# Reordering the routing and the first items of a linear-attention and expert kernel

## The chip, the cores and the metric

The kernel runs on one core of one Trainium2 chip. A core has five engines [...]: TensorE (PE, matmuls; the loading of its stationary operand is listed as PEld), VectorE (DVE), ScalarE (ACT), GpSimd (POOL) and SyncE (SP, which here only issues DMAs). The metric is the device time of one execution in microseconds (us). Three runs of the kernel before took 386.9, 387.04 and 388.13 us; their median is 387.04.

## The reference

Two blocks follow one another, all in float32. The first is a linear attention with a decayed state (4 batches, 8 heads, 768 tokens, head size 48):

```
for t in range(S):
    cur = einsum('bhd,bhe->bhde', u * k[t], v[t])
    y[t] = einsum('bhd,bhde->bhe', r[t], state + cur)
    state = w * state + einsum('bhd,bhe->bhde', k[t], v[t])
```

Its output, put together over the heads, is `x` (4 x 768 tokens of 384 numbers). The second is a mixture of 8 experts of hidden size 1024. Each token takes its own best expert, or, where a local gate says so, the expert of the token before it:

```
for s in range(S):
    fresh_e = argmax(logits[b, s])
    e = fresh_e if s == 0 or local_gate[b, s] < 0.5 else prev_e
    prev_e = e
    out[b, s] = softmax(logits[b, s])[e] * (relu(x[b, s] @ w1[e]) @ w2[e])
```

## The kernel before

**The attention** works through 16 items, numbered n; an item is one batch and a pair of heads. Its 768 tokens are six chunks of 128. For each item the kernel makes, by name:

- `scale` (POOL): `ke` (keys with their decay to the chunk's end, L217), `pd` (r times k, L221) and from item 3 on `rw` (r with its decay, L234), each as two instructions.
- `keys` (DVE): `kw`, keys over the decay (L241).
- `scores` (PE, L288, and DVE, L290): products of `rw` and `kw`, in two groups g of three chunks; DVE masks them into `am`. The second group's mask is handed back as a function, which `run` calls as `keep()`.
- `own` (PE, L269, and DVE, L273): each token's own term, written to the PSUM tile `y`, then multiplied by v.
- `added` (PE, L253): the sum of k times v of each chunk, into a part of the PSUM tile `mp`; `states` (DVE, L259): a scan over the chunks, which reads these sums and gives the states `S`.
- `inside` (PE, L297): `am` times v, added to `y`; `before` (PE, L310): `rw` times `S`, added to `y`; then ACT copies `y` to `xT` (L314).
- `turn` (PE, L323, and ACT, L325): `xT` transposed back to tokens; after each fourth item ACT sends `x` to memory.
- `logits` and `token_logits` (L336, L342): after each fourth item, the router's logits.

PSUM is tight: there is one `y` tile, so an item's `own` follows the copy of the last item's `y`; and two `pair` tiles, taken in turn by scores, turns and logits, each of which waits for the reader of the one before the last. `ke`, `pd`, `kw`, `am` and `S` have two buffers each. The loads rk (r and k), kv and vT are issued by SP three items ahead.

**The order** is written out by hand in `Attention.run`. [...] From item 5 on the scores are made one item ahead.

**The routing** is woven into the same loop. The tokens are routed in two groups of two batches. The first group's routing (`router...(0)`) runs from item 9 to item 15: `experts_of` finds each token's best expert; `keys` transposes (L690) and `runs` scans (L695) to carry an expert along to later tokens; `turn_runs` (L700, with ACT's copy L701) transposes back; `last` (L707) spreads the last token's result; `one_hot` (L713 to L720), `counts` (L727, L728), `ranks` (L734 to L746), `slots` (L775 to L778), `columns` (L783), `numbers` (L788) and `places` (L794) give each token its place in its expert's list; `summed` (L801), `copied` (L807) and `head` (L811 to L832) make the list of the tokens to gather, and `heads()` starts the gather on POOL (L1048). In `ranks` the places at which the second group's tokens go on are written too (L744, L745). The second group's routing runs in `Experts.routing`, beside the first expert's matmuls.

**The experts** follow: ten units of gathered tokens, each with two matmul stages, the larger ones with fewer products and more sums on DVE. The weights come by DMA two units ahead.

Of the kernel before, what the change touches and what calls it, by code (L numbers as in the profile page):

```python
# [14 lines left out]
Alu = mybir.AluOpType  # L15
# [5 lines left out]
P = 128  # L21
# [5 lines left out]
E, F = 8, 1024  # L27
DK, FK = D // P, F // P
NCH = S // P
NC = B * NCH  # L30
# [7 lines left out]
EARLY = 2  # L38
HEAD = 192
TAIL = 256  # L40
# [10 lines left out]
C2 = NCH // 2  # L51
# [4 lines left out]
def spread(ap, axis, n):  # L56

    a = ap.unsqueeze(axis)
    return a.to_broadcast([n if i == axis else s for i, s in enumerate(a.shape)])


class Attention:
# [145 lines left out]
    def scale(self, n):  # L208

        nc, t = self.nc, self.items[n]  # L210
        t["ke"] = self.two.tile([P, NCH, 2 * DH], F32, name="ke")
        t["pd"] = self.two.tile([P, NCH, P], F32, name="pd")
        t["rw"] = self.four.tile([P, NCH, P], F32, name="rw")
        hp = t["hp"]

        def ke(p):
            nc.gpsimd.tensor_mul(t["ke"][:, p::2], t["k"][:, p::2], spread(self.endT[:, p, hp], 1, C2))  # L217

        def pd(i):
            z = slice(i * C2, (i + 1) * C2)  # L220
            nc.gpsimd.tensor_mul(t["pd"][:, z], t["rT"][:, z], t["kT"][:, z])  # L221

        def rw(i):
            self.decayed(nc.gpsimd, n, slice(i * C2, (i + 1) * C2))


        for what in (pd, ke) if n < 3 else (ke, rw, pd) if n < 5 else (rw, ke, pd):
            for i in range(2):
                what(i)

# [60 lines left out]

    def inside(self, n):
        nc, t = self.nc, self.items[n]
        for c in range(NCH):
            p, c2 = c % 2, c // 2
            for h in range(2):
                nc.tensor.matmul(t["y"][p * DP:(p + 1) * DP, h, c2 * P:(c2 + 1) * P],  # L297
                                 lhsT=t["v"][:, (2 * c + h) * DH:(2 * c + h) * DH + DP],
                                 rhs=t["am"][:, c // 3, h, c % 3], start=False, stop=False, skip_group_check=True)
# [45 lines left out]
    def run(self, router, fetch, heads):  # L345


        def pair(name):
            t = self.banks(name)
            return [t[:, 0], t[:, 1]]  # L350

        M = B * HP

        mp, mp_end = router.mp, 2 * P + 2 + (NCH - 1) * DH

        g = GROUPS[0][1] * HP
        for n in range(M + 1):
            if n + AHEAD - 1 < M:
                self.load(n + AHEAD - 1)
            elif n + 2 == M:  # L360
                fetch()
            if n == 0:
                self.scale(0)
                self.keys(0)
                self.tables()
                self.scores(0, 0)()
                self.scores(0, 1)()
                self.own(0)
                self.nc.scalar.copy(self.first, self.tab[:, 1, 0])
                self.turn_ends(slice(1, HP))  # L370
                self.warm(3)
                self.added(0)
                self.reciprocals(1)
                self.states(0)
                self.scale(1)
                continue
            if n < 3:

                self.keys(n)
                self.inside(n - 1)  # L380
                self.before(n - 1)
                if n == 2:
                    self.turn(0, pair("tp"))
                self.nc.scalar.copy(self.first, self.tab[:, n + 1, 0])
                self.scores(n, 0)()
                keep = self.scores(n, 1)
                self.own(n)
                if n == 1:
                    keep()
                self.added(n)  # L390
                self.states(n)
                if n == 2:
                    keep()
                else:
                    self.reciprocals(2)
                self.scale(n + 1)
                continue
            if n < M:
                self.turn(n - 2, pair("tp"))
                if n == g + 3:  # L400
                    router.turn_runs(0, mp[:, mp_end:])
                if n == g + 4:
                    router.counts(0, [mp, mp[:, E * NC // 2:]])
                if n == 3:
                    self.added(3)
                    self.reciprocals(3)
                if n < 5:
                    self.keys(n)
                if n > 3:
                    self.added(n)  # L410
            if n == g + 3:
                router.last(0, mp[:, mp_end:])
            if n < M:
                self.states(n)
            if n > HP and n % HP == 1:
                self.token_logits(n // HP - 1, pair("lq")[0])
            if n == 3:
                self.chooser()
            if n == g + 1:
                router.experts_of(0, (0,))  # L420
            if n == g + 3:
                router.one_hot(0)
            if n == g + 4:
                router.ranks(0, (0,))
            if n == g + 5:
                router.slots(0)
                router.columns(0)
            if n == g + 6:
                router.numbers(0)
            if n == M:  # L430
                router.shares(0)
            if n + 1 < M:
                self.scale(n + 1)
            if 3 <= n < 6:
                router.constants(n - 3)
            if n == M:
                self.turn(M - 2, pair("tp"))
            self.inside(n - 1)
            self.before(n - 1)
            if n == 6:  # L440
                router.cast()
            if n == M:
                break
            if n == g + 7:

                router.summed(0, 0)
                router.copied(0)

            ahead = n if n < 5 else n + 1
            if ahead < M:  # L450
                self.scores(ahead, 0)()
                keep = self.scores(ahead, 1)
            if n % HP == 0:

                keep()
                self.own(n)
                self.logits(n // HP - 1, pair("lp")[0])
                if n == 4:
                    self.keys(5)
                    self.scores(5, 0)()  # L460
                    self.scores(5, 1)()
                    self.keys(6)
                else:
                    self.keys(n + 2)
                if n == g + 4:
                    router.ranks(0, (1,))
            else:
                self.own(n)
                if 4 < n < M - 2:
                    self.keys(n + 2)  # L470
                if ahead < M:
                    keep()
            if n == g + 1:
                router.experts_of(0, (1,))
            if n == g + 2:
                router.keys(0, mp)
                router.runs(0)
            if n == g + 5:
                router.places(0, 0)
            if n == g + 6:  # L480
                router.places(0, 1)
            if n == g + 7:
                router.head(pair("tb")[0])
                heads()
        self.inner.close()


# [79 lines left out]
class Router:  # L567
# [162 lines left out]
    def ranks(self, i, parts=(0, 1)):  # L730

        nc, g, n = self.nc, self.g[i], self.g[i]["nc"]
# [5 lines left out]
        if 1 in parts:  # L738
            if i == 0:

                nc.vector.tensor_scalar(g["far"], g["pos"][:, :EARLY], float(HEAD), float(TAIL - HEAD), Alu.is_ge, Alu.mult)
                nc.vector.tensor_tensor(g["pos"][:, :EARLY], g["pos"][:, :EARLY], g["far"], op=Alu.add)
                base, end = self.g[1]["ext"][:, :, 0:1], g["exc"][:, :, n:]
                nc.vector.tensor_copy(base, end)  # L744
                nc.vector.tensor_scalar(base[:, :EARLY], end[:, :EARLY], float(TAIL - HEAD), float(TAIL), Alu.add, Alu.max)  # L745
            nc.vector.tensor_tensor(g["pos"], g["pos"], g["oh"], op=Alu.mult)  # L746

    def blocks(self):

# [52 lines left out]
                                  rhs=g["ohq"][:, c], start=(i == 0 and what == 0 and c < 4), stop=True,  # L802
                                  skip_group_check=True)

    def copied(self, what):
        self.rows = self.tl(f"rows{what}", [P, P]) if not hasattr(self, "rows") else self.rows
        self.nc.scalar.copy(self.rows, self.mp[:, what * P:(what + 1) * P])  # L807

    def turned(self, bank):

# [3 lines left out]
    def heads(self, table, out):  # L814
        self.nc.vector.tensor_reduce(out, table[:, :EARLY, :2], axis=AX.X, op=Alu.add)
# [160 lines left out]
class Experts:  # L976
# [345 lines left out]
    def routing(self, s):  # L1322

        r, bank = self.router, self.bank
        if s == 0:
            r.experts_of(1)
            r.shares(1)
            r.gates(0)
        if s == 1:
# [386 lines left out]
```

## Time and profile before

| | |
|---|---|
| median of three runs | 387.04 us |
| profiled execution | 387.78 us |
| its span, first to last instruction | 386.1 us |
| PE busy | 368.5 us, 95% |
| DVE busy | 250.4 us, 65% |
| POOL busy | 150.6 us, 39% |
| attention | about 0 to 118 us |
| experts | about 118 to 380 us |
| HBM traffic | 193 GB/s over the span, 410 GB/s and more in the first 45 us |

A line of the timeline reads: start in us, length in us, engine, line of the kernel, operation, what it writes and reads, shape, count; in brackets the idle time of the engine before it, and who ended that. Lines of one engine that follow one another and are alike are merged. The page's clock row is the share of full clock, in tenths, that TensorE was granted in each of 40 equal slices (9.65 us each).

### The profile page before, as it was taken

What the parts mean: (1) busy time and instruction counts of PE and PEld (TensorE: products, weight loads), DVE (VectorE), ACT (ScalarE), POOL (GpSimd) and SP (SyncE); (2) the same over time, 40 slices, a digit from 0 to 9 for tenths busy, and PEclk for the clock granted to TensorE, in tenths of its full rate; (3) what the DMA queues carried; (4) which work ended last, traced back from release to release, by engine and by line L of the source; (5) the groups of instructions that cost most, each with busy time, mean ns of one, the idle gap of its engine ahead of it and who ended that gap; (6) DMA issues with size and microseconds to landing.
All of it is one profiled execution on the core that took longest, in us unless ns stands there. A gap on an engine that the chain in (4) does not pass through costs nothing. (4 is left out here: it accounts for less than half of the span.)

```text
span 386.1 us, 9699 instructions
## 1 busy us (share of the span) xinstructions
PE 368.5 (95%) x3858; PEld 326.4 (85%) x3858; DVE 250.4 (65%) x718; ACT 107.4 (28%) x293; POOL 150.6 (39%) x212
## 2 busy tenths in 40 slices
PE   7998999989999999999999999999999999999992
PEld 6775777667768998998999999999999999999971
DVE  6887678959944654587557757758757758556400
ACT  4132232313232111322322233234224234222220
POOL 8769999849222031511333212212413213012022
PEclk9999999989999999999999999999999999999998
DMA  7999999969404891740552146145146146064011
GB/s 253 412 411 410 406 371 322 373 233 342 153 22 144 345 361 39 252 185 23 185 184 103 42 170 220 60 171 205 60 180 225 38 166 230 17 208 174 2 37 37
DMA packets 17478, 74.97 MB, mean 194 GB/s; under 512 B 2730, under 2 KB 6587, under 8 KB 14865
## 3 DMA queue, kind: packets, MB, share of 16 engines
q1 hardware_dynamic: 10048, 56.89, 39.6%
q0 software_dynamic: 3424, 9.52, 7.6%
q10 hardware_dynamic: 3952, 7.87, 5.5%
q8 instruction: 32, 0.52, 0.6%
q14 instruction: 22, 0.17, 0.2%
HBM read 64.83 MB, written 9.51 MB: 193 GB/s over the span
## 5 line engine op out<-in xcount | busy, mean ns | idle before, releaser
L1274 POOL DMA_INDIRECT out_dram<-yo,sid x27 | 26.6, 987 | 102.4 <-ACT yo L1269 79.0
L1125 PE MATMUL h<-exT,w1t 128*128 128x168 f32 (+4 forms) x240 | 54.9, 327 | 0.0
L1129 DVE TENSOR_TENSOR hT<-h,hs 128x168 f32<-128x168 f32 (+3 forms) x60 | 21.0, 351 | 46.6 <-PE h L1125 30.5
L1048 POOL DMA_INDIRECT xg<-x_d,gid x29 | 31.1, 1074 | 39.1 <-DVE sm L883 17.4
L1125 PEld LDWEIGHTS h<-exT,w1t 128*128 128x128 f32 x240 | 41.7, 190 | 0.3 <-issue 0.3
L1075 PE MATMUL h<-exT,w1t 128*128 128x192 f32 (+1 forms) x192 | 38.2, 337 | 0.0
L1194 PE MATMUL y<-factors,sums 128*128 128x192 f32 x168 | 36.8, 326 | 0.0
L290 DVE TENSOR_TENSOR am<-pair,kept 128x768 f32<-128x768 f32 x32 | 30.0, 950 | 9.6 <-PE pair L288 9.2
L221 POOL TENSOR_TENSOR pd<-rk 128x384 f32<-128x384 f32 x32 | 31.4, 1000 | 10.8 <-PE y L269 9.6
L1125 PE MATMUL h<-xs,ws 128*128 128x168 f32 (+4 forms) x144 | 35.2, 326 | 0.0
L1075 PEld LDWEIGHTS h<-exT,w1t 128*128 128x128 f32 x192 | 32.3, 190 | 1.4 <-issue 0.2
L1125 PEld LDWEIGHTS h<-xs,ws 128*128 128x128 f32 x144 | 25.5, 190 | 4.3 <-ACT hs L1132 1.2
L1194 PEld LDWEIGHTS y<-factors,sums 128*128 128x128 f32 x168 | 28.9, 190 | 0.0
L297 PE MATMUL y<-am,kv 128*64 128x128 f32 x384 | 26.7, 284 | 0.8 <-DVE y L273 0.8
L217 POOL TENSOR_TENSOR ke<-kv,endT 128x288 f32<-128x288 f32 x32 | 24.9, 798 | 4.4 <-DMA kv<-in_kv_dram 3.2
L288 PE MATMUL pair<-rw,kw 48*64 48x128 f32 (+1 forms) x768 | 22.9, 249 | 2.4 <-DVE kw L241 1.1
L297 PEld LDWEIGHTS y<-am,kv 128*64 128x64 f32 x384 | 23.1, 141 | 1.3 <-DVE y L273 1.2
L314 ACT COPY xT<-y 128x768 f32<-128x768 f32 (+1 forms) x16 | 12.5, 780 | 39.7 <-PE y L310 39.7
L234 POOL TENSOR_TENSOR rw<-rk,tab 128x384 f32<-128x384 f32 x26 | 23.5, 924 | 0.0
L288 PEld LDWEIGHTS pair<-rw,kw 48*64 48x64 f32 x768 | 19.7, 133 | 4.4 <-issue 2.7
L1194 PE MATMUL y<-w2t,hT 128*128 128x192 f32 x96 | 23.0, 328 | 0.0
L1062 DVE COPY exT<-tp 128x384 f32<-128x384 f32 (+6 forms) x29 | 14.0, 488 | 13.6 <-PE tp L1061 13.4
(279 smaller groups left out, 736.3 us busy)
## 6 DMA issues: line engine op xcount, KB each, us to landing
w1t<-in_w_dram SPq DMA_DIRECT2D x9, 1536.0 KB, 6.7
w2t<-in_w_dram SPq DMA_DIRECT2D x9, 1536.0 KB, 7.7
rk<-in_rk_dram SPq DMA_DIRECT2D x15, 768.0 KB, 8.5
kv<-in_kv_dram SPq DMA_DIRECT2D x16, 584.0 KB, 8.1
vT<-in_vT_dram SPq DMA_DIRECT2D x16, 384.0 KB, 8.0
x_d<-x ACTq DMA_DIRECT2D x4, 1152.0 KB, 8.7
w1t<-in_w_dram ACTq DMA_DIRECT2D x1, 1536.0 KB, 11.1
w2t<-in_w_dram ACTq DMA_DIRECT2D x1, 1536.0 KB
```

Of the source, the lines that this page charges most:

```text
L217: nc.gpsimd.tensor_mul(t["ke"][:, p::2], t["k"][:, p::2], spread(self.endT[:, p, hp], 1, C2))
L221: nc.gpsimd.tensor_mul(t["pd"][:, z], t["rT"][:, z], t["kT"][:, z])
L234: engine.tensor_mul(t["rw"][:, z], t["rT"][:, z], spread(pw, 1, z.stop - z.start))
L288: nc.tensor.matmul(sc[f * DP:(f + 1) * DP, h, i, x:], lhsT=t["kw"][q, c, o * DP:(o + 1) * DP], rhs=t["rw"][q, c, x:], start=True, stop=True)
L290: return lambda: nc.vector.tensor_mul(t["am"][:, g], sc, spread(self.kept[:, g:g + 3], 1, 2))
L297: nc.tensor.matmul(t["y"][p * DP:(p + 1) * DP, h, c2 * P:(c2 + 1) * P], lhsT=t["v"][:, (2 * c + h) * DH:(2 * c + h) * DH + DP], rhs=t["am" ...
L1048: self.nc.gpsimd.indirect_dma_start(out=xg[:n], out_offset=None, in_=self.x_d[:rows], in_offset=bass.IndirectOffsetOnAxis(ap=u["gid"][:n, ...
L1075: nc.tensor.matmul(h[:, :n], lhsT=u["w1"][:, m, kk, :], rhs=u["xT"][:, kk, :], start=(kk == 0), stop=(kk == DK - 1))
L1125: nc.tensor.matmul(out, lhsT=a, rhs=b, start=start and k == 0, stop=stop and k == len(terms) - 1, skip_group_check=True)
L1129: nc.vector.tensor_tensor(out, a, b, op=Alu.add)
L1194: return lambda: nc.tensor.matmul(bank[:, x * half:(x + 1) * half], lhsT=a, rhs=b, start=(j == 0 and x == 0), stop=(j == FK // 2 - 1), ski ...
L1274: self.nc.gpsimd.indirect_dma_start(out=out.rearrange("n (h d) -> (n h) d", h=2) if half else out, out_offset=bass.IndirectOffsetOnAxis(ap ...
```

## The change

Five things are reordered in `Attention.run`, and small functions adapted to it.

1. The routing's `keys` and `runs` move up in item 10, right behind own (L269, L273) and ahead of the product `kw` and the second `am`. `turn_runs` moves down, between `inside` and `before`; `last` and the first part of `one_hot` move behind `before`. `states` of item 11 no longer stands behind `last`. The second part of `one_hot` goes to the end of the item, `counts` and the first part of `ranks` move to item 12's end, behind the logits.
2. `kw` of item 5 is made in item 4's step ahead of `inside`, right behind item 4's `kw` and `S`. In item 3, `added` and `states` move behind `own` and `keep()`; in item 2, `keep()` stands ahead of `states`.
3. The start of the second token group's slots (L744, L745) leaves `ranks` and becomes `carried`, called in the experts.
4. In item 3 POOL makes `rw` ahead of `ke`.
5. `inside` goes through the same twelve matmuls, with the two column halves p of the array in turn.

Besides, in item 15 the list's copy (`copied`) is made by DVE instead of ACT, and the list's transpose and the gather are emitted ahead of `own`.

```
-        for what in (pd, ke) if n < 3 else (ke, rw, pd) if n < 5 else (rw, ke, pd):
+        for what in (pd, ke) if n < 3 else (ke, rw, pd) if n == 4 else (rw, ke, pd):
...
-        for c in range(NCH):
-            p, c2 = c % 2, c // 2
-            for h in range(2):
+        for c2, h in [(c2, h) for c2 in range(C2) for h in range(2)]:
+            for p in range(2):
+                c = 2 * c2 + p
                 nc.tensor.matmul(t["y"][p * DP:(p + 1) * DP, h, c2 * P:(c2 + 1) * P],
...
                 self.own(n)
-                if n == 1:
-                    keep()
+                keep()
                 self.added(n)
                 self.states(n)
-                if n == 2:
-                    keep()
-                else:
+                if n == 1:
                     self.reciprocals(2)
...
             if n < M:
                 self.turn(n - 2, pair("tp"))
-                if n == g + 3:
-                    router.turn_runs(0, mp[:, mp_end:])
-                if n == g + 4:
-                    router.counts(0, [mp, mp[:, E * NC // 2:]])
                 if n == 3:
-                    self.added(3)
                     self.reciprocals(3)
                 if n < 5:
                     self.keys(n)
                 if n > 3:
                     self.added(n)
-            if n == g + 3:
-                router.last(0, mp[:, mp_end:])
-            if n < M:
-                self.states(n)
+                    self.states(n)
+            if n == 4:
+                self.keys(5)
...
-            if n == g + 3:
-                router.one_hot(0)
-            if n == g + 4:
-                router.ranks(0, (0,))
...
             self.inside(n - 1)
+            if n == g + 3:
+                router.turn_runs(0, mp[:, mp_end:])
             self.before(n - 1)
...
+            if n == g + 3:
+                router.last(0, mp[:, mp_end:])
+                router.one_hot(0, (0,))
             if n == g + 7:
                 router.summed(0, 0)
-                router.copied(0)
+                router.copied(0, self.nc.vector.tensor_copy)
+                router.head(pair("tb")[0])
+                heads()
...
                 if n == 4:
-                    self.keys(5)
                     self.scores(5, 0)()
                     self.scores(5, 1)()
                     self.keys(6)
-                else:
+                if n == g + 4:
+                    router.counts(0, [mp, mp[:, E * NC // 2:]])
+                    router.ranks(0, (0,))
+                if n > 4:
                     self.keys(n + 2)
                 if n == g + 4:
                     router.ranks(0, (1,))
             else:
                 self.own(n)
+                if n == g + 2:
+                    router.keys(0, mp)
+                    router.runs(0)
+                if n == 3:
+                    self.added(3)
                 if 4 < n < M - 2:
                     self.keys(n + 2)
                 if ahead < M:
                     keep()
+                if n == 3:
+                    self.states(3)
             if n == g + 1:
                 router.experts_of(0, (1,))
-            if n == g + 2:
-                router.keys(0, mp)
-                router.runs(0)
+            if n == g + 3:
+                router.one_hot(0, (1,))
...
-            if n == g + 7:
-                router.head(pair("tb")[0])
-                heads()
...
-                base, end = self.g[1]["ext"][:, :, 0:1], g["exc"][:, :, n:]
-                nc.vector.tensor_copy(base, end)
-                nc.vector.tensor_scalar(base[:, :EARLY], end[:, :EARLY], float(TAIL - HEAD), float(TAIL), Alu.add, Alu.max)
             nc.vector.tensor_tensor(g["pos"], g["pos"], g["oh"], op=Alu.mult)
+
+    def carried(self):
+        nc, n = self.nc, self.g[0]["nc"]
+        base, end = self.g[1]["ext"][:, :, 0:1], self.g[0]["exc"][:, :, n:]
+        nc.vector.tensor_copy(base, end)
+        nc.vector.tensor_scalar(base[:, :EARLY], end[:, :EARLY], float(TAIL - HEAD), float(TAIL), Alu.add, Alu.max)
...
-    def copied(self, what):
+    def copied(self, what, copy=None):
...
-        self.nc.scalar.copy(self.rows, self.mp[:, what * P:(what + 1) * P])
+        (copy or self.nc.scalar.copy)(self.rows, self.mp[:, what * P:(what + 1) * P])
...
         if s == 0:
             r.experts_of(1)
+            r.carried()
             r.shares(1)
             r.gates(0)
```

Here `g` is 8, so that `g + 2` is item 10 and `g + 4` item 12.

## The prediction

> **What bounds the kernel now.** I read the page first: its engine totals, then its clock row.
>
> ```profile
> span 386.1 us, 9699 instructions
> PE 368.5 (95%) x3858; PEld 326.4 (85%) x3858; DVE 250.4 (65%) x718; ACT 107.4 (28%) x293; POOL 150.6 (39%) x212
> ...
> PEclk9999999989999999999999999999999999999998
> ```
>
> TensorE (PE) is the bound from end to end. It is idle for some 8.7 us between its first and last matmul, and the clock drops in one slice in the middle, 77 to 87 us. The chain of waits is no help: it stops at the last scatter. So I went by the timeline of PE, where each idle time stands beside its releaser. The stage view puts 7.47 busy us into the stretch from 76 to 86 us, at a mean clock of 0.83, and 260.2 of 262 us into the experts' stretch from 118 to 380 us. The experts don't change and have nothing to give; the change lives in the attention part, the first 118 us. There the timeline of PE has three places that the diff touches. The first and largest:
>
> ```profile
> 75.52 0.28 PE L690 MATMUL mp<-ident,key 128*12 128x128 f32 x1
> 75.75 0.79 PE L323 MATMUL pair<-ident,xT 112*128 112x112 f32 x6
> 78.78 0.23 PE L700 MATMUL mp<-ident,run 12*128 12x12 f32 x1 [2.23 <-DVE run L695]
> 79.31 1.04 PE L253 MATMUL mp<-kv,ke 128*48 128x48 f32 x20 [0.30 <-issue]
> 80.28 0.60 PE L707 MATMUL mp<-rn,ident 128*128 128x12 f32 x2
> 80.81 2.48 PE L297 MATMUL y<-am,kv 128*64 128x128 f32 x24
> ```
>
> PE's queue is served in order, so the small transpose L700 of the routing's runs holds everything behind it for 2.23 us. After it L253 takes 1.04 and L297 2.48 us, against 0.65 and 1.58 in every other item. DVE shows why `run` is late:
>
> ```profile
> 75.72 0.97 DVE L273 TENSOR_TENSOR y<-y,vT 128x768 f32<-128x768 f32 x1
> 76.59 0.94 DVE L241 TENSOR_TENSOR kw<-rk,inv 128x768 f32<-128x768 f32 x1
> 77.45 0.95 DVE L290 TENSOR_TENSOR am<-pair,kept 128x768 f32<-128x768 f32 x1
> 78.32 0.40 DVE L695 TENSOR_TENSOR_SCAN run<-mp,seg 12x128 f32<-12x128 f32 x1
> ```
>
> The 0.40 us scan stands behind three large products. The second and third place, items 5 and 13, are PE waiting for DVE again:
>
> ```profile
> 34.05 1.11 PE L288 MATMUL pair<-rw,kw 48*64 48x64 f32 x42 [0.52 <-issue]
> ...
> 38.44 1.24 PE L288 MATMUL pair<-rw,kw 48*64 48x128 f32 x48 [1.10 <-DVE kw L241]
> 40.30 0.41 PE L323 MATMUL pair<-ident,xT 112*128 112x112 f32 x2 [0.62 <-DVE am L290]
> ```
>
> ```profile
> 93.87 0.77 DVE L741 TENSOR_SCALAR far<-pos 128x24 f32<-128x24 f32 x1
> 94.67 0.79 DVE L742 TENSOR_TENSOR pos<-pos,far 128x24 f32<-128x24 f32 x1
> 95.39 0.82 DVE L744 COPY ext<-exc 128x8 f32<-128x8 f32 x1
> 96.24 0.72 DVE L745 TENSOR_SCALAR ext<-exc 128x2 f32<-128x2 f32 x1
> ```
>
> The last four delay item 14's `am`, for which PE waits 0.71 us at 99.25.
>
> [...] its clock record has 3.41 us at 0.5 from 79.34 us, after a window of that length in which PE was idle for 2.5 us; idle times of 1.1 us did not do it. [...] L741, L742, L744 and L745 write 128x24 and less and take 0.72 to 0.82 us, each until one of POOL's instructions ends; L746, 128x96, takes 0.24 with POOL idle. [...] four records of L801 start within 20 ns.
>
> **Routing's wait, item 11.** From one item's L323 to the next takes 5.33 us where nothing waits (46.49 to 51.83); here 10.09 (75.75 to 85.84). L700 and L707 must still be issued: about 0.45 us, since L690 holds 0.23 [...]. So up to 10.09 - 5.33 - 0.45 = 4.3 us can go. In the new order the scan is right behind `y` (76.6 to 77.0 us), and L700 behind L253 and L297, thus at about 75.75 + 0.74 + 0.6 + 1.4 = 78.5. Slack 1.5 us: the wait is gone, and the half clock with it. L707 needs ACT's copy of `rn`, 0.17 us, which has before()'s 0.7 us as cover. Next late: the one-hot operations L714 to L716. They now stand ahead of item 12's first `am`, wanted at 80.5; [...] L323 of item 12 would then wait up to 0.6 us. I take 0.3: **-4.0** (-4.3 to -3.6).
>
> **Array halves in turn.** The 24 records of L297 of one item start in pairs 109 ns apart for five pairs, and then singly 57 and 52 ns apart: both halves already work at once, and the new order can't double anything. First to last start is 1.31 us; L801 and L253, whose halves already alternate, stay paired to their end. Kept paired, L297 would need 1.26: -0.05 x 12 items on PE's path = **-0.6** (-0.8 to 0).
>
> **Items 2 to 5.** These steps nearly cancel. Gains: L253 of item 3 no longer waits for `ke` (0.41 us at 24.46); with `rw` first POOL needs only rk, and has `pd` of item 3 at about 26.6 instead of 28.1; kw of item 5 is made before item 4's `am`, so the 1.10 us go. Followed in order: item 3's scores can't start before its `kw` at 27.2 (before: 27.33), so the 0.41 buys 0.1. Own at 28.5, `y` 29.5 to 30.45, second `am` to 31.3, and only then `S` of item 3, now last, to 31.9. But added(4) overwrites the sums that `S` reads, and stands on PE right behind turn(2), ready at 30.7: **a new wait of 1.25 us**, the queue behind it being all of item 4. Then L253 31.95, L297 32.4, L310 33.9, scores 34.5, own 35.8 (behind ACT's xT), logits 36.6, scores of item 5 at 38.0 (before 38.44, kw long ready), first `am` done at 39.9, L323 39.95 against 40.30: -0.35. That has no room for the 0.52 us at 33.5, for which the profile names no releaser; if it comes again, +0.2. I take **-0.1** (-0.5 to +0.5). The swapped `am` and `S` of item 2 cost DVE the same sum.
>
> **Counts and ranks, items 12 and 13.** L744 and L745 leave (1.54 us on DVE); in the experts, with POOL's products over, they take about 0.06 to 0.17 each beside PE's matmuls: nothing. But L735 and L737 (0.63 + 0.26) come behind own(12), and must wait for L727 and L728, now behind the logits: with own(12) starting at T, ACT has copied the counts at T+3.1, L737 ends T+4.0, kw T+5.0, L741 to L746 T+6.4, `S` T+7.05, slots (1.4) T+8.45, `am` T+9.4. Before, L323 came at T+9.21 with the counts' 0.42 us spent ahead of T: a gain of 0.2. Against it L718 and L720 now stand ahead of item 13's `am` while POOL makes `rw`: 0 to 0.6 us, on the logits. Sum **+0.1** (-0.3 to +0.7).
>
> **Item 15.** The rows' copy moves from ACT to DVE (about 0.3 us, as L807's 0.27) and L811 ahead of own(15): own starts at about 110.3 instead of 109.88, and `y` at 111.3 instead of 110.87, behind L815 to L832: +0.4 on the wait at 111.59. The gather starts 1.3 us earlier; the expert's transposes at 116.65 take 0.91 us, which I read as 0.3 of waiting for its second tile: -0.3. Sum **+0.1** (-0.3 to +0.5). SP's loads keep their order; those that wait for buffers are issued earlier with PE's steps, and land 4 us and more before use.
>
> **Sum.** -4.0 - 0.6 - 0.1 + 0.1 + 0.1 = -4.5. The profiled execution took 387.78 us (span 386.1 and 1.7 around it): 383.3. It lies 0.74 above the median of 387.04. If the lower runs escaped the half clock [...], 383.3 stands; if the 0.74 is noise, 382.5. I say **383.1 us**, a ratio of 0.990.
>
> **Rivals.**
> - *Half is given back* (chance 0.2): the wait goes, but the top ends hold: +0.5, +0.7, +0.5 and no gain of the array's halves, with a wait of 0.6 at item 12: -3.6 + 1.7 = -1.9, some 385.5. For it: DVE has 5.8 us of work in items of 5.3 there.
> - [...] (slower, 0.07): the routing's small operations, moved to where POOL always works, each wait for one of its 0.98 us instructions, as L741 to L745 did. Eight of them (L715, L716, L718, L720, L735, L741, L742, L776) at 0.75 us more is 6 us of DVE time ahead of `am` of items 12 to 14; with about 1 us hidden, 5 us on PE, and 0.5 slower: about 388. It decides once more than six are held so. Against: L681, L682 and L746 were not held.
> - *Nothing measurable* (0.08): the median runs had no half clock [...]: near 386.5.
> - *The wait stays*, because `run` is still late: under 0.02, with 1.5 us of slack.
>
> **How the numbers follow.** The main case has 0.65 and 381.5 to 384.8; with half given back, the range is 381.2 to 386.4. A difference within 0.3% (1.2 us) is about what a measurement of this kernel can't tell from none: faster 0.84, same 0.09, slower 0.07.
>
> **What would show it.** Right: no L700 row with idle time, no slice of lower PEclk in the middle, L253 and L297 of item 11 at 0.65 and 1.5 us; an idle time of about 1.2 us before item 4's L253, released by S L259; none before item 5's scores; 0.3 to 0.5 more before inside(15). Wrong: idle times over 1 us before L323 or L336 of items 12 to 14 released by `am`, with small DVE rows of 0.7 to 1 us ahead; L297 unchanged at 1.58; or a second drop of the clock.

## The result and the profile after

Over 22 runs of each the changed kernel takes 385.39 us and the kernel before 387.48 us: a ratio of 0.9941, with a 95% interval of 0.9918 to 0.9964. The ratios here and below leave out a run that met a slower state of the chip, and are not the quotients of two medians. The kernel is faster, by 2.1 us where 4 were forecast. The profiled execution of the changed kernel took 384.17 us against 387.78, and is the fastest of its 22 runs, so the two profiles differ by 3.6 us, more than the medians do. Both gaps, 3.6 against 4.5 and 2.1 against 3.6, have to be explained.

The page of the kernel after, engine totals and clock row:

```profile
span 382.4 us, 9699 instructions
PE 366.8 (96%) x3858; PEld 324.6 (85%) x3858; DVE 249.3 (65%) x719; ACT 107.2 (28%) x292; POOL 150.5 (39%) x212
...
PEclk9999999999999999999999999999999999999998
```

The slice of lower clock in the middle is gone. PE is idle for 6.6 us between its first and last matmul, against 8.7. The timeline of PE around the routing's wait:

```profile
75.46 0.79 PE L323 MATMUL pair<-ident,xT 112*128 112x112 f32 x6
76.69 0.66 PE L253 MATMUL mp<-kv,ke 128*48 128x48 f32 x20 [0.44 <-issue]
77.15 1.53 PE L297 MATMUL y<-am,kv 128*64 128x128 f32 x24
78.92 0.23 PE L700 MATMUL mp<-ident,run 12*128 12x12 f32 x1 [0.25 <-DVE inc L713]
...
82.10 0.79 PE L323 MATMUL pair<-ident,xT 112*128 112x112 f32 x6
```

The wait of 2.23 us before L700 is gone, and L253 and L297 take 0.66 and 1.53 us instead of 1.04 and 2.48. But two short idle times are new: 0.44 us before L253 and 0.25 before L700. DVE shows what ends them:

```profile
76.19 0.40 DVE L695 TENSOR_TENSOR_SCAN run<-mp,seg 12x128 f32<-12x128 f32 x1
76.52 0.92 DVE L241 TENSOR_TENSOR kw<-rk,inv 128x768 f32<-128x768 f32 x1
...
78.23 0.63 DVE L259 TENSOR_TENSOR_SCAN S<-step,mp 128x240 f32<-128x240 f32 x1
```

L695 ends at 76.59, and L253 starts at 76.69. L259 ends at 78.86, and L700 starts at 78.92. Both DVE operations read `mp`, and both matmuls write `mp`, in other columns. The releasers that the profile prints ("issue", `inc`) are not the cause: in all seven profiles with this order L253 starts 0.10 us after L695's end and L700 0.06 us after L259's, while the idle time before L253 varies from 0.44 to 0.72 us.

Items 2 to 5, on PE's timeline:

```profile
32.34 0.66 PE L253 MATMUL mp<-kv,ke 128*48 128x48 f32 x20 [1.72 <-POOL pd L221]
...
40.24 0.79 PE L323 MATMUL pair<-ident,xT 112*128 112x112 f32 x6 [0.34 <-DVE am L290]
```

This is the new wait of item 4's L253, 1.72 us long. The POOL operation named is not what ended it: L259 of item 3 ran from 31.59 to 32.23 on DVE. The 1.10 us before item 5's scores and the 0.52 us at 33.5 are gone, and L323 of item 5 starts within 0.06 us of where it did.

Items 12 and 13. PE's timeline before, where L253 of item 13 follows at once:

```profile
92.99 0.79 PE L323 MATMUL pair<-ident,xT 112*128 112x112 f32 x6
93.71 0.65 PE L253 MATMUL mp<-kv,ke 128*48 128x48 f32 x20
```

And after, on the timelines of PE and then of DVE:

```profile
87.69 1.50 PE L336 MATMUL pair<-xT,wp 128*32 128x384 f32 x16 [0.29 <-DVE am L290]
...
91.31 0.66 PE L253 MATMUL mp<-kv,ke 128*48 128x48 f32 x20 [0.93 <-DMA w1t<-in_w_dram]
```

```profile
90.80 0.26 DVE L737 TENSOR_TENSOR pos<-exc,mp 128x96 f32<-128x96 f32 x1
...
91.84 0.17 DVE L741 TENSOR_SCALAR far<-pos 128x24 f32<-128x24 f32 x1
92.04 0.18 DVE L742 TENSOR_TENSOR pos<-pos,far 128x24 f32<-128x24 f32 x1
```

Here an idle time of 0.93 us is new. L737 reads L728's product from `mp` until 91.06. In the trace DVE's semaphore is counted up at 91.07; PE's sequencer passes L253's wait for it right after, and checks two further semaphores by 91.26, without a stay. The DMA named arrived during that check. In the five profiles with this order L253 starts 0.26 us (once 0.31) after L737's end, while the releaser printed is a DMA, POOL or ACT. L741 and L742, which took 0.77 and 0.79 us before, now take 0.17 and 0.18.

Set against the profile before, by PE's positions:

| stretch | before | after | difference |
|---|---|---|---|
| start to L323 of item 5 | 40.30 | 40.24 | -0.06 |
| to L323 of item 11 | 35.45 | 35.22 | -0.23 |
| to L323 of item 12 (routing's wait) | 10.09 | 6.64 | -3.45 |
| to L323 of item 14 (counts and ranks) | 14.12 | 14.64 | +0.52 |
| to L323 of item 15 | 5.34 | 5.68 | +0.34 |
| to the first expert's first product | 13.14 | 13.07 | -0.07 |
| experts, to the end of the span | 267.66 | 266.91 | -0.75 |

### The profile page after: what moved, and what is told of

Same layout as the page of the kernel before. It is cut to its first block, busy times and chain, and to the rows that moved or that the text cites. A ratio compares the mean times of both kernels' runs of the same rounds, so it can differ in the third digit from the quotient of the medians.

```text
span 382.4 us, 9699 instructions
## 1 busy us (share of the span) xinstructions
PE 366.8 (96%) x3858; PEld 324.6 (85%) x3858; DVE 249.3 (65%) x719; ACT 107.2 (28%) x292; POOL 150.5 (39%) x212
## 5 line engine op out<-in xcount | busy, mean ns | idle before, releaser
L297 PE MATMUL y<-am,kv 128*64 128x128 f32 x384 | 25.1, 276 | 1.0 <-DVE y L273 1.0
L297 PEld LDWEIGHTS y<-am,kv 128*64 128x64 f32 x384 | 21.1, 137 | 1.9 <-DVE y L273 1.3
```

## The experiments

The theory after the result had four parts. (1) The wait of L700 and its half clock are the gain. (2) Part of it is given back to waits between PE and DVE through the one PSUM tile `mp`. (3) The new wait of 1.7 us in item 4 can let the clock fall in its turn, so that one profile is not typical. (4) The alternation of the array's halves is worth 0.05 us per item. The rival to (2) and (3) was that POOL's instructions hold up DVE's, as L741 took 0.77 us until one of them ended, and the whole attention part is slower than it looks; the rival to (1) was that the wait alone counts and the half clock costs nothing measurable.

The kernel before had a median of 389.4 us (48 runs) beside the first four kernels, 388.36 (41) beside the next four, and 388.82 (11) beside the last two. Each ratio is against the kernel before on the same chip. The first and the third of these sets ran on one chip, the second on another.

### One part alone

**The array's halves alone**, in the kernel before:

```
-        for c in range(NCH):
-            p, c2 = c % 2, c // 2
-            for h in range(2):
+        for c2, h in [(c2, h) for c2 in range(C2) for h in range(2)]:
+            for p in range(2):
+                c = 2 * c2 + p
```

> Part 5 alone: the kernel before with the two column halves of inside() in turn. If the halves already work at once (first theory), L297 is 1.53 us instead of 1.58 in the items where nothing waits, an item lasts 5.28 instead of 5.33, and the time falls by 0.6 us (0.998). If alternating them makes a second half work that was idle (rival), L297 falls by a quarter or more, 0.3 us an item, 4 us in all.

Measured: 388.66 us (14 runs), a ratio of 0.9996 (0.9958 to 1.0033). The median says nothing on 0.6 us, but PE's timeline does:

```profile
46.23 0.79 PE L323 MATMUL pair<-ident,xT 112*128 112x112 f32 x6
47.45 1.53 PE L297 MATMUL y<-am,kv 128*64 128x128 f32 x24
51.51 0.80 PE L323 MATMUL pair<-ident,xT 112*128 112x112 f32 x6
```

An item takes 5.28 us here and 5.33 before (46.49 to 51.83), L297 1.53 and 1.58. The 0.05 us per item is real, and small.

**The early items alone** (items 2 to 5, with `rw` first in item 3):

```
                 self.own(n)
-                if n == 1:
-                    keep()
+                keep()
...
                 if n == 3:
-                    self.added(3)
                     self.reciprocals(3)
...
+            if n == 4:
+                self.keys(5)
...
                 self.own(n)
+                if n == 3:
+                    self.added(3)
...
+                if n == 3:
+                    self.states(3)
```

> Parts 2 and 4 alone (items 2 to 5, r first in item 3). First theory: what kw of item 5 gains, 1.1 us, the wait of item 4's L253 for item 3's S takes back, 1.7 us; the 0.5 us without a releaser at 33.5 is what stood there instead. L323 of item 5 at 40.2 to 40.3 as before, time unchanged within 0.3 us. Rival (the moves gain what they remove): 1.5 us less, L323 of item 5 near 38.8.

Measured: 389.94 us (22 runs), a ratio of 1.0002 (0.9981 to 1.0024). No gain can be seen. Its profile (390.2 us of span), on PE's timeline:

```profile
32.36 0.66 PE L253 MATMUL mp<-kv,ke 128*48 128x48 f32 x20 [1.73 <-issue]
32.82 2.62 PE L297 MATMUL y<-am,kv 128*64 128x128 f32 x24
```

Right behind the new wait, L297 takes 2.62 us instead of 1.53: the clock record has 0.5 for 3.41 us from 33.08. L323 of item 5 comes at 41.84, some 1.5 us later than in the kernel before and than expected.

**The routing alone** (parts 1 and 3 of the change):

> Parts 1 and 3 alone (the routing's order and the moved slots; list copy and gather as before, halves and items 2 to 5 as before). First theory (a wait removed, with its half clock): item 11 is 3.5 us shorter, items 12 to 14 are 0.9 longer, time 2.5 us less in a run where the clock fell before, about 1.2 us less in one where it did not. Rival (only the clock counted, the wait would have been made up later): nothing is gained against runs of before whose clock did not fall, and the medians differ by less than 0.7 us.

Measured: 386.16 us (7 runs), a ratio of 0.9897 (0.985 to 0.9944). That is 4.0 us, more than the 2.5 expected, on a chip where the clock of the kernel before fell often (its mean lay between 0.976 and 0.993); the rival is excluded. The changed kernel had 0.9914 on this chip (below), so the routing alone can be the whole of the gain. This kernel has the same idle times as the changed one, 0.56 us before L253 of item 11, 0.23 before L700, 0.93 before L253 of item 13. They belong to the routing's new places, not to the early items.

Its profiled run is the slowest of the seven (389.26 us), and shows something else. PE's timeline:

```profile
38.17 1.24 PE L288 MATMUL pair<-rw,kw 48*64 48x128 f32 x48 [1.10 <-DVE kw L241]
40.02 0.99 PE L323 MATMUL pair<-ident,xT 112*128 112x112 f32 x6 [0.62 <-DVE am L290]
...
43.31 2.89 PE L297 MATMUL y<-am,kv 128*64 128x128 f32 x24
...
49.25 0.79 PE L323 MATMUL pair<-ident,xT 112*128 112x112 f32 x6
```

These are the old waits of item 5, 1.10 and 0.62 us as in the kernel before. Here the clock record has 0.5 for 6.83 us from 40.48, and L323 of item 6 comes 9.23 us after item 5's; in the profile before, with the same two waits at full clock, it was 6.19. So the early items of the kernel before can lose the clock too.

**The keys of item 5 alone**, the one edit of the early items without a wait of its own:

```
+            if n == 4:
+                self.keys(5)
...
                 if n == 4:
-                    self.keys(5)
                     self.scores(5, 0)()
```

> The kernel before with kw of item 5 made in item 4's step, and nothing else. First theory: the 1.10 us before item 5's scores go and nothing takes their place, since DVE is idle from 32.9 to 34.7 us; 1.1 us less, 0.997. Rival (the wait comes back at item 5's L323, which waits for am): less than 0.4 us.

Measured: 387.47 us (22 runs), a ratio of 0.9961 (0.9938 to 0.9984), so some 1.5 us (0.6 to 2.4). L323 of item 5 starts at 38.88 instead of 40.30, in agreement, and the wait does not come back.

### The half clock by itself

In the kernel before, the six transposes of item 11's turn are issued four times over, with the same operands and results. PE then works through most of the wait, which ends no sooner.

```
-    def turn(self, n, banks):
+    def turn(self, n, banks, times=1):
...
-        for h in range(2):
+        for h in [h for _ in range(times) for h in range(2)]:
...
-                self.turn(n - 2, pair("tp"))
+                self.turn(n - 2, pair("tp"), 4 if n == g + 3 else 1)
```

> The kernel before, with item 11's six transposes (L323) issued four times over, into the same place with the same values: PE works while it would wait for the routing's scan, and the wait's end is where it was. If the half clock is a price of the idle time on top of the wait (first theory): no clock of 0.5 after 79 us, L253 0.65 and L297 1.58 us in item 11, L269 of item 11 1.3 to 1.5 us sooner than 85.03, and the time up to 1.4 us less; in the median less, for the runs in which the clock did not fall anyway. If the clock falls for another reason (rival): L297 2.48 again and no gain.

Measured: 387.32 us (19 runs), a ratio of 0.995 (0.9924 to 0.9977). PE's timeline:

```profile
76.31 2.52 PE L323 MATMUL pair<-ident,xT 112*128 112x112 f32 x24 [0.37 <-DVE am L290]
79.23 0.23 PE L700 MATMUL mp<-ident,run 12*128 12x12 f32 x1 [0.39 <-DVE run L695]
79.76 0.66 PE L253 MATMUL mp<-kv,ke 128*48 128x48 f32 x20 [0.30 <-POOL rw L234]
```

L700 starts no earlier than before (79.23 against 78.78), but L253 takes 0.66 us instead of 1.04, and from L700 to item 12's L323 (84.78 instead of 85.84) it takes 5.55 us instead of 7.06. More work made the kernel faster by 0.5%, about 1.9 us (0.9 to 3.0; up to 1.4 was expected): this is the half clock's share of the wait's cost, and the rival to (1) falls. Six of the 19 runs still have a mean clock of 0.987 to 0.989 and take 389.6 to 390.5 us; where the clock fell in them is not known, but item 5's two waits are still in this kernel.

### The changed kernel again

> The changed kernel once more, beside the next one on the same chip. Ratio to before 0.992 to 0.996; runs with a mean clock of 0.991 or less in about a third of the cases, and those 1.3 us slower for each 3.4 us of half clock.

Measured: 385.8 us (6 runs), a ratio of 0.9914 (0.988 to 0.9948). This time the profiled run (384.8 us of span) met the half clock behind item 4's wait. PE's timeline:

```profile
32.35 1.01 PE L253 MATMUL mp<-kv,ke 128*48 128x48 f32 x20 [1.73 <-POOL ie_i L613]
33.10 2.85 PE L297 MATMUL y<-am,kv 128*64 128x128 f32 x24
...
41.87 0.79 PE L323 MATMUL pair<-ident,xT 112*128 112x112 f32 x6 [0.34 <-DVE am L290]
```

The same kernel, with L253 at 32.35 against 32.34, has L323 of item 5 at 41.87 against 40.24: 1.63 us lost behind a wait of the same length. So part (3) of the theory is shown: the same wait costs 1.7 us in one run and over 3 in another. Only this one of the six runs has a clock below 0.993, where a third was expected.

Of the changed kernel's 22 runs in the result, 14 have a mean clock of 0.993 and more and a median of 384.9 us, and 8 have 0.986 to 0.991 and a median of 386.7. Of the 1.2 us between the profile and the median, 0.5 is thus due to the runs of lower clock; the other 0.7 is that the profiled run is the fastest even among the 14. That the clock of the 8 fell in item 4 is likely, but they left no profile.

The clock records show what stood ahead of the falls. In the profile before, the record changes 75.09 us after its start, which is 22 times the 3.41 us that the fall lasted; in the changed kernel's first profile it changes once, 372.05 us after its start, 109 times 3.41, behind the last matmul. Cut into such stretches from the record's start to the last matmul, the profile before has 2.53 us of idle PE in the stretch ahead of its fall and at most 1.04 in any other. The changed kernel's first profile has 1.72 us in the stretch from 30.43 to 33.84, after which the clock stayed, and at most 0.93 in any other; the runs do not say why. In the second profile the stretch before the fall is 29.01 to 32.42, with 1.73 us. In one pair of profiles short waits seem to have added up: item 5's two waits came to 1.72 us in one stretch with the routing alone, and the clock fell; in the profile before they were divided into 1.04 and 0.68, and it did not.

### Parts put back

**The early items as before**, with item 5's keys still early, in the changed kernel:

```
-        for what in (pd, ke) if n < 3 else (ke, rw, pd) if n == 4 else (rw, ke, pd):
+        for what in (pd, ke) if n < 3 else (ke, rw, pd) if n < 5 else (rw, ke, pd):
...
                 if n == 3:
+                    self.added(3)
                     self.reciprocals(3)
...
-                    self.states(n)
+                self.states(n)
...
-                if n == 3:
-                    self.added(3)
...
-                if n == 3:
-                    self.states(3)
```

> The changed kernel with added(3), states(3), item 2's keep() and item 3's ke and rw back in their old places; kw of item 5 stays early. First theory (the 1.72 us that item 4's L253 waits for item 3's S is paid for that move alone): that wait is gone, the 0.41 us for ke is back, none of 1.1 before item 5's scores; L323 of item 5 near 39.2 us instead of 40.24, time 1.0 us below the changed kernel, and fewer runs with a fallen clock; about 0.987 to 0.991 of before. Rival (the wait only moves on): another wait of about 1 us in items 4 and 5, and 0.994 as the changed kernel.

Measured: 384.56 us, a ratio of 0.9892 (0.9845 to 0.9939). All six runs lie between 384.46 and 384.98 with a clock of 0.993 and more. The 1.72 us wait is gone and the old one of 0.41 us is back; L323 of item 5 comes at 39.30. The 0.93 us before L253 of item 13 stays.

**The counts and the one-hot operations back as well**: besides the above, `counts` is emitted behind item 12's turn again, the first part of `ranks` behind its first `am`, and `one_hot` in one piece:

```
+                if n == g + 4:
+                    router.counts(0, [mp, mp[:, E * NC // 2:]])
...
+            if n == g + 4:
+                router.ranks(0, (0,))
...
-                router.one_hot(0, (0,))
+                router.one_hot(0)
```

> The same, and also counts, the first part of ranks and the whole of one_hot in the old places relative to the attention (counts behind item 12's turn, one_hot behind last). First theory (item 13's L253 waits for DVE's L737 because both use the PSUM tile mp): its 0.93 us and the 0.29 us before the logits are gone, up to 0.5 us come at item 12's L323 for the one-hot operations ahead of am; 0.5 to 0.9 us less than with the items alone put back. Rival (L253 waits for something else, a load or ke): the wait of 0.9 us stays.

Measured: 383.43 us (6 runs, 382.84 to 383.96), a ratio of 0.9859 (0.9813 to 0.9906), the best here. PE's timeline:

```profile
77.70 0.66 PE L253 MATMUL mp<-kv,ke 128*48 128x48 f32 x20 [0.72 <-issue]
...
83.38 0.79 PE L323 MATMUL pair<-ident,xT 112*128 112x112 f32 x6 [0.26 <-DVE am L290]
...
91.20 0.65 PE L253 MATMUL mp<-kv,ke 128*48 128x48 f32 x20
```

The idle times of 0.93 and 0.29 us in items 12 and 13 are gone, and 0.26 stands before item 12's L323 in their place. L741 and L742 (L740 and L741 in this kernel) take 0.82 and 0.79 us again and hold nobody up, so the shorter ones of the changed kernel bought nothing. The two lengths go with POOL: here it makes `rw` from 91.22 to 92.91 while they run, and in the changed kernel it is idle from 91.35 to 92.11. The wait of item 11's L253 for the scan L695 remains, now 0.72 us.

**Item 15 back too**: from the last kernel, the copy of the list is made by ACT again and the list's transpose and the gather stand behind `own`.

```
-                router.copied(0, self.nc.vector.tensor_copy)
-                router.head(pair("tb")[0])
-                heads()
+                router.copied(0)
...
+            if n == g + 7:
+                router.head(pair("tb")[0])
+                heads()
```

> The changed kernel with items 2 and 3, counts and one_hot put back, and item 15's list copy and gather in the old place and order too. The moved tail came out even in the profiles (0.5 us more before inside of item 15, 0.4 us less at the logits and 0.1 at the gathered tokens). First theory (even): item 15's y and inside 0.4 us sooner, the first expert's start within 0.2 us of the moved version, ratio to before 0.985 to 0.988. Rival (the earlier gather is worth something): 0.4 us or more slower to the first expert's matmuls.

Measured: 384.25 us (6 runs), a ratio of 0.9876 (0.9839 to 0.9914). On the same chip the changed kernel took 385.8. From item 15's L323 to the first expert's product it takes 12.97 us, the kernel with the edit 13.06: the last `inside` starts 0.48 us sooner, the gather later, and the expert's transposes wait 0.36 us for its rows. In the profiles the edit of item 15 moves the end of this stretch by 0.09 us, which is as good as nothing.

### Filling item 4's wait

In the changed kernel, item 4's transposes are issued three times, so that PE is idle there for less.

```
-                self.turn(n - 2, pair("tp"))
+                self.turn(n - 2, pair("tp"), 3 if n == 4 else 1)
```

> The changed kernel with item 4's six transposes (turn of item 2, L323) issued three times, same place and values: the wait of item 4's L253 is filled with work and ends when it did. If this wait is a place where the clock falls in a part of the runs (first theory): no clock of 0.5 within 30 to 42 us, fewer runs with a mean clock below 0.993 than 8 of 22, the median 0.3 to 0.8 us below the changed kernel's, the fastest run the same. Rival (the runs differ for other causes): the same spread as the changed kernel.

Measured: 386.41 us (20 runs, 385.67 to 389.2), a ratio of 0.9952 (0.9927 to 0.9978). The clock did what was expected: the idle time falls to 0.57 us, and only one of 20 runs has a mean clock below 0.993, against 8 of the 22 of the result, which were not taken beside it. The median did not follow: 0.3 to 0.8 us less than the changed kernel was expected, and the ratio is no better than its 0.9941. PE's timeline:

```profile
32.38 0.66 PE L253 MATMUL mp<-kv,ke 128*48 128x48 f32 x20 [0.57 <-issue]
...
45.78 1.76 PE L269 MATMUL y<-pd,w_t 48*64 48x384 f32 x8
```

L253 starts where it did, but L269 of items 5, 6 and 8 is stretched, to 1.76 us here and 1.34 and 1.60 later, from 0.87, with no releaser and no lower clock, for some 2 us in all. What stretches it is open. So this kernel speaks for the idle time as what makes the clock fall, and says nothing on what the fall costs.

## Why the prediction was right and wrong

The direction and the main mechanism were right; the likeliest time, 383.1 us, was 2.3 too low, and 385.39 lies above the main case's 381.5 to 384.8. The median lies nearly on the rival "half is given back" (385.5), but that is luck in part: the wait went and part of it was given back, as the rival says, yet of its terms only the one for the counts came (+0.52 for +0.7); the rest was given back to waits that no rival names.

**Routing's wait, item 11**: right in kind, -3.45 measured, 0.05 of it the halves', for -4.0. The scan ended at 76.6 as forecast, L700 no longer waits for it, and the half clock is gone. The step that failed is "Slack 1.5 us: the wait is gone". It looked only at L700, the reader of `run`. The scan also *reads* `mp`, and L253, now queued behind it, *writes* `mp`. `mp` is one PSUM tile of 128 x 512 floats, and the sums, the transposed keys, the runs and the counts are all parts of it. In the trace L253 waits 0.44 us for L695 and L700 0.25 for L259, in columns that do not overlap. What it is about `mp` that orders them was not shown: no run put the sums or the keys into another tile. The wait expected instead, of L323 of item 12 for the held one-hot operations (0.3), did not come. L700 and L707 took some 0.67 us instead of the 0.45 set down (6.64 less an item's 5.28 and the two waits of 0.44 and 0.25).

**Array halves in turn**: right, 0.05 us per item, seen alone and in the change.

**Items 2 to 5**: the cancelling was right (-0.06 measured in the profile for -0.1), with the new wait at 1.72 us instead of 1.25, since item 3's `y` began at 29.85 and not at 29.5, and the unnamed 0.52 us gone. The failed part is the price of a wait: the step took the sum of one profile for the median. "Idle times of 1.1 us did not do it" is true of that profile alone. With the routing alone the same 1.10 and 0.62 us did it and cost 3.0 us more, and the new 1.7 us does it in some runs, and the fall adds 1.6 us. In the prediction's trace PE was idle for 2.5 us in the 3.41 us ahead of the fall; in the second profile of the changed kernel 1.73 us stood ahead of one. Without the 1.7 us wait (the early items as before) all six runs keep a clock of 0.993 and more, and the profile's L323 of item 5 comes 0.94 us earlier.

**Counts and ranks, items 12 and 13**: mis-sized, +0.52 for +0.1. The named risk, L718 and L720 held on DVE, came as 0.29 us before the logits (they took 0.50 and 0.97 us beside POOL's `rw`, and 0.26 and 0.17 before, with POOL idle). The larger part, 0.93 us before L253 of item 13, was not in the sum, and is the tile `mp` again: L737 still reads L728's product from the tile that L253 is to write. What leaving out L744 and L745 brings was not tried by itself.

**Item 15**: the two halves of the step, +0.4 and -0.3, were seen as +0.48 and -0.39 in the last two kernels put back. Not in the sum was item 14, +0.34: DVE has two `am`, a column product `ohq`, `S` and `val` ahead of the `am` that L323 waits for. As I read the two profiles, the 0.71 us by which PE waited at item 14 before had given DVE that time; no run tests it.

**The sum**: to the first expert's product -2.95 us instead of -4.5. The 1.5 missing are 0.6 in item 11, 0.5 in items 12 and 13 with their halves, 0.3 from item 14 to the first expert, and 0.1 before item 11. Another 0.75 in the experts was in nobody's sum, and most of it is luck of one run: before one product of the first experts (L1162 before, L1166 after) the profile before waits 0.48 us, the changed kernel's second profile 0.50, and its first not at all; the other 0.27 is not explained. From the profile to the median, 384.17 to 385.39, 0.5 is the runs of lower clock, and 0.7 the fastest run standing for all.

The rival in which eight small operations wait for POOL did not come about: only L718 and L720 of them were held where somebody waited, for 0.29 us. What failed is the place: POOL was idle when L715, L716, L741 and L742 began, and they took 0.17 to 0.18 us. "Nothing measurable" and "the wait stays" are excluded by the interval and by L700's row.

## What to carry to other kernels

When an instruction is moved, list what it reads as well as what it makes: here a read of a PSUM tile that PE writes in other columns held PE's next write three times, for 0.44, 0.25 and 0.93 us. Add up PE's idle times that lie close together: in the five stretches of 3.41 us read off here with 1.72 us and more (up to 2.53), the clock fell after four, and this cost 1.5 to 3.0 us on top of the waits. Compare the clock of many runs, not two profiles. Here the changed kernel without the two moves that made new waits is the fastest of all (0.9859).

## What the runs showed that was not expected

- An idle time of 1.72 or 1.73 us, the same to 0.01 us, was followed by 3.41 us at half clock in one profile of the changed kernel and in that of the early items alone, and by full clock in the other profile of the changed kernel.
- Adding matmuls that compute nothing new made the kernel before 0.5% faster.
- The mean clocks of 41 runs of the kernel before lie in four groups, near 0.993, 0.989, 0.985 and 0.977. Runs of the two highest take 386.7 to 387.9 us, of the third 388.4 to 389.3, of the last 390.6 to 392.1: the falls come in steps, and a median depends on how many a chip happens to show. The two highest groups take the same time: the mean counts the time behind the last matmul too, in which every profile has half clock for 2.3 to 5.5 us, so 0.004 of it can mean nothing.
- The stretched L269 of the filled wait has no releaser and no lower clock, and stays unexplained.
